# Key rows of a query block reordered to 32 keys, 24 summaries, 64 keys, in a fused window-attention and two-MoE-layer kernel

## Chip, core and metric

The kernel runs on one core of one Trainium2 chip. The metric is device microseconds of one execution, lower is better. Inputs and outputs are float32.

## What is computed

Attention over 2 batches of 8 heads with 768 tokens of 64 values each. A query sees the keys less than 16 tokens away, and 24 summaries: for each run of 32 tokens the maximum of its keys and the mean of its values. Two feed-forward layers follow. The reference, cut to what matters:

```python
block, window = (32, 16)
k_sum = k.reshape(B, H, nb, block, D).max(axis=3)
v_sum = v.reshape(B, H, nb, block, D).mean(axis=3)
scores_l = scale * np.matmul(q, k.transpose(0, 1, 3, 2))
mask_l = np.abs(pos[:, None] - pos[None, :]) < window
scores_s = scale * np.einsum('bhsd,bhnd->bhsn', q, k_sum) + np.log(block)
a = softmax(concat([where(mask_l, scores_l, -1e9), scores_s]))
x = a @ concat([v, v_sum])              # tokens x 512
h = np.maximum(x @ w_in, 0.0); x = h * h @ w_out
xn = rms_norm(x) * rms_g
out = (silu(xn @ w_gate) * (xn @ w_val)) @ w_out2
```

The weights arrive as float64 and are turned into float32 pairs on the chip.

## The kernel before

**Attention.** Tokens are worked on in 12 groups of 128 (6 to a batch), each as two query blocks of 64. For a block, 120 key rows are used: 96 keys of its window and the 24 summaries of its batch. `kT` holds the keys of a batch with the head dimension on the partitions; the rows of neighbouring blocks overlap in it, so that one slice of 120 columns is a block's whole key list. The list reads 16 keys, 12 summaries, 64 keys, 12 summaries, 16 keys: the two half sets of summaries alternate in the gaps between the blocks' keys. `vx` is the same list of values, with the 120 rows on the partitions and four slots, two blocks to a group.

For each group: `scores` (tiles `s`, PE), `softmax` (adding a mask, maximum, exponential, sum, scaling; tiles `t`, `mx`, `sm`; DVE and ACT), `ptrans` (transposes of `t` into `pps`, copied by ACT to `pT`), `av` (product with `vx` into `xps`), and `split_xs`, which makes from `xps` a rounded part `xhi` (ACT) and the rest `xlo` (DVE) for the next layer. A batch is prepared by `prep_k` (transposes of `kr` into `kps`, the maxima into `ksum` on DVE, a copy to `kT` on ACT), `prep_kend` (the summaries into the gaps of `kT`, DVE), `qprep` (`qr` through `qps` to `qT`) and `vmean` (24 means of the values from `vr` by a matmul, copied to `vm` on ACT).

**Values.** `vload` brings the keys' values of a group to `vx`, three DMAs to a block: 16, 64 and 16 rows. `vmfix` brings the means to the two 12-row places of each slot by DMA from `vm`, 4 DMAs for batch 0 and 8 for batch 1. All DMAs are issued from SP's queue, in order.

**Weights.** `Units` loads float64 weights (`raw_wi`, `raw_wo`, 512 KB each) and converts them: `conv_a` two ACT operations (L177, L178), `conv_b` four DVE operations (L184, L185, L188, L191), `split` one ACT cast (L197) and one DVE subtraction (L198). Of the first eight weight tiles, one is loaded near the start and seven are issued behind the first `vmfix` (`after("vmfix")`, L625).

**Order.** The program text gives the order of pieces; a scheduler then sets the instruction order of each engine, and each engine runs its instructions in that order. PE starts with batch 0's attention, then mixes the first feed-forward round (`h_pair` into tiles `h`, `y_pair` into tiles `y`, for token pairs `k_` of 256) with the attention of the later groups, to about 160 us; from there to the end it runs the feed-forward layers alone. Batch 1 is prepared in the round `k_ == 0`, and its means in the round `k_ == 1`, between `av(5)` and group 7.

Of the kernel before, what the change touches and what calls it, by code (L numbers as in the profile page):

```python
# [32 lines left out]
def tile_window_attention_moe_moe2(  # L33
# [25 lines left out]
    GAP = NB // 2  # L59
    NK = NB + KW  # L60
    STEP = QT + GAP
    NW1 = S // QT
    K0 = WIN + GAP
    K1 = K0 + STEP
    LK = WIN + (NW1 + 1) * GAP + S + WIN
# [31 lines left out]
    def constants():  # L97
# [33 lines left out]
        nc.gpsimd.memset(last[QT:P, K1:NK], NEG)  # L131
# [186 lines left out]
    def prep_k(b, c):  # L318
# [23 lines left out]
    def prep_kend(b, a):  # L342
        ksum = state[b]
        gaps = kT[:, :, WIN : WIN + NW1 * STEP].rearrange("d p (n s) -> d p n s", s=2 * STEP)
        half = ksum[:, :, GAP * a : GAP * (a + 1)]
        nc.vector.tensor_copy(
            gaps[:, :, :, STEP * a : STEP * a + GAP],
            half.unsqueeze(2).to_broadcast([P, NPAIR, NW1 // 2, GAP]),
        )
# [20 lines left out]
    def vmean(b, c):  # L370

        if c == 0:
            state["vmps"] = psA(f"vmean{b}", [NB, DM])
        ps = state["vmps"]
# [8 lines left out]
        if c == NC2 - 1:  # L383
            vm = ap_.tile([NB, DM], F32, tag="vm", name=f"vm{b}", bufs=1)
            nc.scalar.copy(vm, ps)
            state["vm"] = vm
            state[("vsum", b)] = True

    def vmfix(i0, n):

        vt = vx.rearrange("k (i u) h d -> k u i (h d)", u=2)
        for u in range(2):
            for j, a in ((WIN, u), (K0 + QT, 1 - u)):
                rows = state["vm"][GAP * a : GAP * (a + 1)]
                mark["vmfix"] = nc.sync.dma_start(
                    vt[j : j + GAP, u, i0 : i0 + n], rows.unsqueeze(1).to_broadcast([GAP, n, DM])
                )
# [300 lines left out]
    for k_ in range(NK2):  # L698
# [26 lines left out]
        if k_ == 0:  # L725
# [3 lines left out]
            prep_kend(1, 0)  # L729
            prep_kend(1, 1)  # L730
# [130 lines left out]
```

## Time and profile before

| | us |
|---|---|
| median of 3 runs | 676.23 |
| lowest, highest | 674.78, 677.02 |
| the profiled execution | 675.57 |
| its span on the core | 673.9 |
| PE busy in the span | 646.7 (96%) |
| DVE busy | 403.7 (60%) |
| ACT busy | 305.2 (45%) |
| POOL busy | 4.0 (1%) |

Engines: PE is TensorE, PEld its weight loads, DVE VectorE, ACT ScalarE, POOL GpSimd, SP the engine that issues the DMAs ("SPq" is its queue). Times count from the start of the span. An engine runs its instructions in order, so that one that waits holds up all behind it. The busy shares are means over stages: the first 125 us, where attention and the first feed-forward round mix, look different from the rest, and a change is to be read in its own stage. "PEclk" is the granted clock of PE as a share of 2.4 GHz; 0.50 is the level of 1.2 GHz.

### The profile page before, as it was taken

The numbers are of one execution on the slowest core, as the hardware profiler recorded it, in microseconds if no ns is written. First come the engines' busy times: TensorE is split into PE (matmuls) and PEld (weight loads), VectorE is DVE, ScalarE is ACT, GpSimd is POOL, SyncE is SP. The second block draws the span as 40 slices with busy tenths as digits, with TensorE's granted clock in tenths as the row PEclk, the third lists the DMA queues.
The fourth block names the chain that finished last, engine by engine and source line by source line (L and its number), as shares of the span: only waits on it lengthen the run. The fifth ranks groups of instructions, "written<-read, shape, count | busy, mean of one in ns | idle before, by whom it ended". The sixth has DMA issues, their size and how long they took to land.

```text
span 673.9 us, 9361 instructions
## 1 busy us (share of the span) xinstructions
PE 646.7 (96%) x3644; PEld 534.0 (79%) x3644; DVE 403.7 (60%) x733; ACT 305.2 (45%) x637; POOL 4.0 (1%) x25
## 2 busy tenths in 40 slices
PE   7668988999999999999999999999999999999997
PEld 5457957888888888888888888888888888888885
DVE  4799858565999669826665795189713172313132
ACT  4497558365775447416352773167511131111110
POOL 2000000000000000000000000000000000000000
PEclk9779998899999999999999999999999999999999
DMA  9677565221712314001022252014300000001011
GB/s 243 145 251 174 151 176 162 57 62 39 243 63 71 118 61 127 32 1 62 1 94 63 64 181 69 1 31 157 124 1 1 0 1 0 1 1 62 1 62 63
DMA packets 78188, 54.22 MB, mean 80 GB/s; under 512 B 46080, under 2 KB 72704, under 8 KB 78144
## 3 DMA queue, kind: packets, MB, share of 16 engines
q1 hardware_dynamic: 78144, 53.62, 26.9%
q8 instruction: 29, 0.48, 0.3%
q14 instruction: 15, 0.12, 0.1%
HBM read 50.07 MB, written 3.15 MB: 79 GB/s over the span
## 4 chain that ended last, share of the span: by engine, by line
PE 88%; SPq 4%; DVE 2%; DMA 2%; ACT 2%; issue 1%; DVEq 0%; ACTq 0%
PE y L532 19%; PE h L511 19%; PE v L511 15%; PE g L511 15%; PE z L532 14%; SPq L406 2%; PE xps L490 2%; PE s L420 2%; DMA raw_wi<-in_moe_w_in_dram 1%; PE pps L469 1%; SPq L305 1%; ACT t L449 1%; PE xps L502 1%; PE qps L366 1%; SPq L294 1%
## 5 line engine op out<-in xcount | busy, mean ns | idle before, releaser
L511 PE MATMUL h<-xhi,w_wi 128*128 128x512 f32 (+1 forms) x480 | 134.8, 354 | 2.5 <-ACT w_wi L197 1.7
L532 PE MATMUL y<-w_wo,hhi 128*128 128x512 f32 x384 | 119.8, 396 | 1.6 <-ACT hhi L522 1.4
L807 DVE TENSOR_TENSOR sg<-v,sg 128x512 f32<-128x512 f32 x36 | 24.8, 690 | 131.2 <-PE v L511 131.2
L511 PEld LDWEIGHTS h<-xhi,w_wi 128*128 128x128 f32 x480 | 86.5, 194 | 15.3 <-ACT w_wi L197 2.1
L511 PE MATMUL v<-xhi,w_wv 128*128 128x512 f32 x288 | 94.8, 390 | 0.0
L511 PE MATMUL g<-xhi,w_wg 128*128 128x512 f32 x288 | 94.6, 390 | 0.0
L532 PE MATMUL z<-w_wp,hhiz 128*128 128x512 f32 x288 | 88.1, 390 | 0.0
L511 PE MATMUL h<-xlo,w_wi 128*128 128x512 f32 (+1 forms) x240 | 85.2, 355 | 1.8 <-DVE xlo L481 1.8
L532 PEld LDWEIGHTS y<-w_wo,hhi 128*128 128x128 f32 x384 | 72.6, 191 | 16.9 <-ACT hhi L522 1.6
L532 PE MATMUL y<-w_wo,hlo 128*128 128x512 f32 x192 | 74.7, 399 | 0.0
L805 ACT ACTIVATE sg<-g 128x512 f32<-128x512 f32 x36 | 21.6, 599 | 102.3 <-PE g L511 100.0
L511 PEld LDWEIGHTS v<-xhi,w_wv 128*128 128x128 f32 x288 | 54.1, 188 | 11.2
L511 PEld LDWEIGHTS g<-xhi,w_wg 128*128 128x128 f32 x288 | 54.0, 188 | 11.1
L532 PEld LDWEIGHTS z<-w_wp,hhiz 128*128 128x128 f32 x288 | 54.0, 188 | 11.1
L659 ACT ACTIVATE r<-h 128x512 f32<-128x512 f32 x48 | 28.7, 597 | 66.2 <-PE h L511 65.9
L511 PE MATMUL v<-xlo,w_wv 128*128 128x512 f32 x144 | 56.1, 390 | 0.0
L511 PE MATMUL g<-xlo,w_wg 128*128 128x512 f32 x144 | 56.1, 389 | 0.0
L532 PE MATMUL z<-w_wp,hloz 128*128 128x512 f32 x144 | 55.4, 390 | 0.0
L522 ACT CAST hhiz<-sg 128x512 fp32r<-128x512 f32 x36 | 22.4, 621 | 68.3 <-DVE sg L807 68.0
L511 PEld LDWEIGHTS h<-xlo,w_wi 128*128 128x128 f32 x240 | 46.6, 194 | 8.4 <-DVE xlo L481 2.4
L660 DVE TENSOR_TENSOR r<-h,r 128x512 f32<-128x512 f32 x48 | 32.8, 684 | 33.0 <-ACT r L659 32.8
L532 PEld LDWEIGHTS y<-w_wo,hlo 128*128 128x128 f32 x192 | 36.2, 191 | 7.4 <-DVE mx L447 0.2
(125 smaller groups left out, 895.7 us busy)
## 6 DMA issues: line engine op xcount, KB each, us to landing
raw_wi<-in_moe_w_in_dram SPq DMA_DIRECT2D x16, 512.0 KB
raw_wo<-in_moe_w_out_dram SPq DMA_DIRECT2D x16, 512.0 KB
raw_wg<-in_moe_w_gate_dram SPq DMA_DIRECT2D x12, 512.0 KB
raw_wv<-in_moe_w_val_dram SPq DMA_DIRECT2D x12, 512.0 KB
raw_wp<-in_moe_w_out_dram SPq DMA_DIRECT2D x12, 512.0 KB
kr<-in_k_dram SPq DMA_DIRECT2D x12, 256.0 KB
qr<-in_q_dram SPq DMA_DIRECT2D x12, 256.0 KB
vr<-in_v_dram SPq DMA_DIRECT2D x6, 512.0 KB
```

The source lines that it names most:

```text
L294: nc.sync.dma_start(t.rearrange("p h e d -> p h (e d)"), src[b, :, 2 * P * c : 2 * P * (c + 1), :].rearrange("h (p e) d -> p h (e d)", e=2),)
L305: nc.sync.dma_start(t[:, j].rearrange("p (h d) -> p h d", h=H), src[b, :, o : o + P, :].rearrange("h p d -> p h d"),)
L406: nc.sync.dma_start(vx[j : j + n, i0 + u], v[b, :, o : o + n, :].rearrange("h s d -> s h d"))
L420: mark[("s", g)] = nc.tensor.matmul(sl[e][QT * u : QT * u + QT, p, :], qT[rr, p, QT * u : QT * u + QT], kT[rr, p, o : o + NK], start=True, ...
L490: nc.tensor.matmul(ps[QT * e : QT * e + QT, o : o + QT], vx[:, (2 * g + u) % NVX, 2 * p + e, :], pT[:, e * NPAIR + p, QT * u : QT * u + QT ...
L511: nc.tensor.matmul(ps, a_, b_, start=(i == 0), stop=(i == tot - 1))
L522: nc.scalar.copy(hi[:, 0:n], s[:, 0:n])
L532: nc.tensor.matmul(y, a_[:, ms], b_, start=(first and i == 0), stop=(last and i == 2))
L659: nc.scalar.activation(t, ps, AF.Relu)
L660: nc.vector.tensor_tensor(t, ps, t, op=ALU.mult)
L805: nc.scalar.activation(t, psg, AF.Silu)
L807: nc.vector.tensor_tensor(t, psv, t, op=ALU.mult)
```

## The change

A block's list of key rows becomes 32 keys, 24 summaries, 64 keys. The gaps of `kT` now hold all 24 summaries each. `prep_k` writes the keys with two ACT copies instead of one (12 more copies in all). `prep_kend` copies the summaries once on DVE for four blocks and once on POOL for eight (batch 0), or once on POOL for all twelve (batch 1). `vload` needs two DMAs to a block, of 32 and 64 rows. The means' rows stand in one place of `vx` (rows 32 to 55), so `vmean` is computed on those partitions and engines write the rows: DVE from PSUM for the first two slots of batch 0, POOL from `vm` for the others. The DMAs of `vmfix` are gone, and with them the order that put the seven weight loads behind them: these are now issued behind the second tile of queries. The masks follow the new order.

```diff
-            nc.scalar.copy(
-                kT[:, 2 * hf : 2 * hf + 2, K0 : K0 + NW1 * STEP]
-                .rearrange("d p (n s) -> d p n s", s=STEP)[:, :, nb1 * c : nb1 * (c + 1), 0:QT],
-                ps.rearrange("d p (n s) -> d p n s", s=QT),
-            )
+            nc.scalar.copy(kv[:, :, :, 0:WIN], pv[:, :, :, 0:WIN])
+            nc.scalar.copy(kv[:, :, :, WIN + NB : QT + NB], pv[:, :, :, WIN:QT])
...
+    def prep_kend(b, eng, w0, w1):
+        gaps = kT[:, :, WIN : WIN + NW1 * STEP].rearrange("d p (n s) -> d p n s", s=STEP)
+        eng.tensor_copy(
+            gaps[:, :, w0:w1, WIN : WIN + NB],
+            state[b].unsqueeze(2).to_broadcast([P, NPAIR, w1 - w0, NB]),
+        )
...
+            if b == 0:
+                nc.vector.tensor_copy(vrows(0, 2), ps.unsqueeze(1).to_broadcast([NB, 2, DM]))
             nc.scalar.copy(vm, ps)
...
+    def vmput(i0, n):
+        nc.gpsimd.tensor_copy(vrows(i0, n), state["vm"].unsqueeze(1).to_broadcast([NB, n, DM]))
...
-    prep_kend(0, 1)
+    prep_kend(0, nc.vector, 0, 4)
+    prep_kend(0, nc.gpsimd, 4, NW1)
...
-    vmfix(0, NVX // 2)
-    with after("vmfix"):
-        units1.load(8)
+    vmput(2, 2)
+    units1.load(8)
...
-            vmfix(0, 1)
+            vmput(0, 2)
...
-                vmfix(1, 1)
+                vmput(2, 2)
...
-            prep_kend(1, 0)
-            prep_kend(1, 1)
+            prep_kend(1, nc.gpsimd, 0, NW1)
```

**The start, SP's queue.** The rows show the end of the first loads of `vx` and the weights' issue, first before (`vm_292` are batch 0's means):

```order
L406 DMA vx<-in_v_dram 64x8x64
L406 DMA vx<-in_v_dram 16x8x64
L305 DMA qr_141<-in_q_dram 128x8x64 x2
L395 DMA vx<-vm_292 12x2x512 x4
L162 DMA raw_wi_298<-in_moe_w_in_dram 128x4x256
L162 DMA raw_wi_300<-in_moe_w_in_dram 128x4x256
L162 DMA raw_wi_302<-in_moe_w_in_dram 128x4x256
L166 DMA raw_wo_304<-in_moe_w_out_dram 128x1024
```

and in the changed kernel:

```order
L403 DMA vx<-in_v_dram 32x8x64
L403 DMA vx<-in_v_dram 64x8x64
L304 DMA qr_137<-in_q_dram 128x8x64 x2
L161 DMA raw_wi_296<-in_moe_w_in_dram 128x4x256
L161 DMA raw_wi_298<-in_moe_w_in_dram 128x4x256
L161 DMA raw_wi_300<-in_moe_w_in_dram 128x4x256
L165 DMA raw_wo_302<-in_moe_w_out_dram 128x1024
```

The four DMAs of the means are gone, the weights stand right behind the queries, and 8 loads of `vx` stand ahead of them instead of 12.

**Batch 1's means, SP's queue.** Before, from the end of the load of group 7's values (`vm_1093` are batch 1's means, `raw_wi_1515` and the rest the next weights):

```order
L406 DMA vx<-in_v_dram 16x8x64
L162 DMA raw_wi_1515<-in_moe_w_in_dram 128x4x256
L162 DMA raw_wi_1517<-in_moe_w_in_dram 128x4x256
L166 DMA raw_wo_1978<-in_moe_w_out_dram 128x1024
L395 DMA vx<-vm_1093 12x512 x8
L162 DMA raw_wi_1980<-in_moe_w_in_dram 128x4x256
L166 DMA raw_wo_1982<-in_moe_w_out_dram 128x1024
```

and in the changed kernel:

```order
L403 DMA vx<-in_v_dram 64x8x64
L161 DMA raw_wi_1493<-in_moe_w_in_dram 128x4x256
L161 DMA raw_wi_1495<-in_moe_w_in_dram 128x4x256
L165 DMA raw_wo_1954<-in_moe_w_out_dram 128x1024
L161 DMA raw_wi_1956<-in_moe_w_in_dram 128x4x256
L165 DMA raw_wo_1958<-in_moe_w_out_dram 128x1024
```

Eight DMAs between two weight loads are gone.

**The same place, ACT and DVE.** ACT before (`t_1015` is the softmax tile of group 6, `t_1123` that of group 7, `x_wi_1852` the first step on the second of the new weights):

```order
L480 CAST xhi_1_929<-xps_5_1067 128x4x128
L449 ACTIVATE t_1015,sm_1017<-t_1015,mx_1016 128x120 x8
L197 CAST w_wi_1856<-x_wi_1718 128x512
L177 ACTIVATE x_wi_1852<-raw_wi_1515 128x512
L385 COPY vm_1093<-vmean_1086 24x512
L178 ACTIVATE u_wi_1853<-raw_wi_1515 128x512
```

and now:

```order
L446 ACTIVATE t_1007,sm_1009<-t_1007,mx_1008 128x120 x8
L477 CAST xhi_1_923<-xps_5_1059 128x4x128
L384 COPY vm_1085<-vmean_1078 24x512
L196 CAST w_wi_1832<-x_wi_1694 128x512
L446 ACTIVATE t_1110,sm_1112<-t_1110,mx_1111 128x120 x8
L176 ACTIVATE x_wi_1828<-raw_wi_1493 128x512
```

The copy of the means and the exponentials of group 7 moved ahead of the new weights' first step. Some rows further on ACT, before (`pT_1295` are group 7's transposed weights of attention, `t_1243` is group 8's softmax tile):

```order
L659 ACTIVATE r_2_2_1333<-h_2_2_1308 128x512
L178 ACTIVATE u_wo_2025<-raw_wo_1982 128x512
L470 COPY pT_1295<-pps_0_1296 120x512
L470 COPY pT_1295<-pps_1_1302 120x512
L449 ACTIVATE t_1243,sm_1245<-t_1243,mx_1244 128x120 x8
```

and now:

```order
L177 ACTIVATE u_wo_2001<-raw_wo_1958 128x512
L467 COPY pT_1277<-pps_0_1278 120x512
L656 ACTIVATE r_2_2_1315<-h_2_2_1290 128x512
L446 ACTIVATE t_1225,sm_1227<-t_1225,mx_1226 128x120 x8
L467 COPY pT_1277<-pps_1_1284 120x512
```

The second half of group 7's `pT` moved behind the eight exponentials of group 8. DVE before, from the second add of group 6 to group 5's `xlo`:

```order
L443 TENSOR_TENSOR t_1015<-s_6_992,mask_first 128x480
L184 TENSOR_SCALAR x_wi_1718<-x_wi_1718 128x512
L447 TENSOR_REDUCE mx_1016<-t_1015 128x8
L185 TENSOR_SCALAR x_wi_1718<-x_wi_1718 128x512
L481 TENSOR_TENSOR xlo_1_930<-xps_5_1067,xhi_1_929 128x4x128
```

and now:

```order
L440 TENSOR_TENSOR t_1007<-s_6_986,mask_first 128x480
L444 TENSOR_REDUCE mx_1008<-t_1007 128x8
L440 TENSOR_TENSOR t_1110<-s_7_1088,mask_mid 128x480
L183 TENSOR_SCALAR x_wi_1694<-x_wi_1694 128x512
L184 TENSOR_SCALAR x_wi_1694<-x_wi_1694 128x512
L187 SCALAR_TENSOR_TENSOR x_wi_1694<-raw_wi_1491,x_wi_1694 128x512
L440 TENSOR_TENSOR t_1110<-s_7_1089,mask_mid 128x480
L190 ISA x_wi_1694<-x_wi_1694,u_wi_1695 128x1024
L444 TENSOR_REDUCE mx_1111<-t_1110 128x8
L454 TENSOR_SCALAR sm_1009<-sm_1009 128x8
L478 TENSOR_TENSOR xlo_1_924<-xps_5_1059,xhi_1_923 128x4x128
```

Group 5's `xlo`, which the next `h` products need, moved behind both adds and the maximum of group 7; on PE the means' matmuls stand between the two halves of group 7's scores.

## Rows read from the trace of the kernel before

**Rows 1.** The page: busy time, and the granted clock in 40 slices.

```profile
PE 646.7 (96%) x3644; PEld 534.0 (79%) x3644; DVE 403.7 (60%) x733; ACT 305.2 (45%) x637; POOL 4.0 (1%) x25
PEclk9779998899999999999999999999999999999999
```

**Rows 2.** The page: the chain that ended last, shares by engine.

```profile
PE 88%; SPq 4%; DVE 2%; DMA 2%; ACT 2%; issue 1%; DVEq 0%; ACTq 0%
```

**Rows 3.** By stage, us busy: PE, PEld, DVE, ACT, POOL; then clock, DMA share, GB/s.

```profile
20.00:28.00 8.00, 2.46 (x11) 1.93 (x10) 7.76 (x20) 3.87 (x14) 0.00 (x0) 0.80 0.54 121
28.00:38.00 10.00, 10.00 (x148) 8.55 (x147) 5.21 (x11) 6.74 (x23) 0.00 (x0) 0.82 0.83 272
38.00:52.00 14.00, 8.12 (x40) 7.27 (x38) 13.60 (x28) 12.47 (x35) 0.00 (x0) 0.64 0.74 204
52.00:70.00 18.00, 15.64 (x198) 12.97 (x198) 18.00 (x33) 13.06 (x34) 0.00 (x0) 1.00 0.77 182
70.00:88.00 18.00, 18.00 (x149) 15.65 (x148) 12.46 (x21) 10.29 (x19) 0.00 (x0) 1.00 0.54 129
...
98.00:100.40 2.40, 0.41 (x4) 0.16 (x3) 0.56 (x2) 1.25 (x3) 0.00 (x0) 1.00 1.06 390
...
110.00:112.50 2.50, 0.69 (x5) 0.45 (x5) 2.50 (x4) 1.26 (x3) 0.00 (x0) 1.00 1.05 329
112.50:124.50 12.00, 12.00 (x82) 9.68 (x83) 8.34 (x13) 7.16 (x23) 0.00 (x0) 0.57 0.49 133
124.50:160.00 35.50, 35.50 (x352) 31.23 (x352) 17.59 (x28) 18.64 (x55) 0.00 (x0) 1.00 0.19 46
```

**Rows 4.** Timeline of SP's queue: start, duration, DMAs of a run.

```profile
13.66 8.72 SPq L406 DMA_DIRECT2D vx<-in_v_dram  x12
22.42 1.06 SPq L305 DMA_DIRECT2D qr<-in_q_dram  x2
...
29.39 1.61 SPq L162 DMA_DIRECT2D raw_wi<-in_moe_w_in_dram  x3
...
90.18 4.34 SPq L406 DMA_DIRECT2D vx<-in_v_dram  x6
94.62 0.94 SPq L162 DMA_DIRECT2D raw_wi<-in_moe_w_in_dram  x2
...
100.29 6.27 SPq L395 DMA_DIRECT2D vx<-vm  x8
106.68 0.49 SPq L162 DMA_DIRECT2D raw_wi<-in_moe_w_in_dram  x1
```

**Rows 5.** Waits from 56 to 130 us: total, times, longest.

```profile
ACT u_wi L178 <- DMA raw_wi<-in_moe_w_in_dram: 2.3, 1, 2.3
...
PE pps L469 <- ACT vm L385: 2.0, 1, 2.0
```

**Rows 6.** Timeline of PE and ACT at three places.

```profile
26.10 1.09 PE L366 MATMUL qps<-ident,qr 128*128 128x128 f32 x4 [5.54 <-DMA qr<-in_q_dram]
...
90.54 5.33 PE L379 MATMUL vmean<-vr,ind 128*24 128x512 f32 x12
...
99.15 0.66 ACT L177 ACTIVATE x_wi<-raw_wi 128x512 f32<-128x512 f32 x1 [3.09 <-DMA raw_wi<-in_moe_w_in_dram]
```

**Rows 7.** Groups by line and shape: busy, mean ns of one.

```profile
L449 ACT ACTIVATE t<-t,mx 128x120 f32<-128x120 f32 x72 | 27.4, 384 | 8.5 <-DVE mx L447 8.5
...
L447 DVE TENSOR_REDUCE mx<-t 128x8 f32<-128x960 f32 x7 | 8.0, 1146 | 0.1
...
L336 ACT COPY kT<-kps 128x512 f32<-128x512 f32 x12 | 7.0, 586 | 7.5 <-DVE ksum L331 7.5
...
L346 DVE COPY kT<-ksum 128x288 f32<-128x288 f32 x4 | 1.2, 308 | 0.1
...
L125 POOL COPY mask_mid<-um 64x16 f32<-64x16 f32 x2 | 0.4, 194 | 0.1
...
L127 POOL COPY mask_first<-mask_mid 128x120 f32<-128x120 f32 x1 | 0.3, 282 | 0.1
```

More of the change, by code (lines that the diff above doesn't have):

```diff
@@ L58, in tile_window_attention_moe_moe2 @@
     KW = QT + 2 * WIN
-    GAP = NB // 2
     NK = NB + KW
-    STEP = QT + GAP
+    STEP = QT + NB
     NW1 = S // QT
-    K0 = WIN + GAP
-    K1 = K0 + STEP
-    LK = WIN + (NW1 + 1) * GAP + S + WIN
+    G0 = 2 * WIN
+    K1 = G0 + NB
+    LK = NW1 * STEP + G0
     GPB = S // P
@@ L122, in constants @@
         nc.gpsimd.memset(mid, math.log(BLK))
-        for j, n, o in ((0, WIN, 0), (K0, QT, WIN), (K1, WIN, WIN + QT)):
+        for j, n, o in ((0, G0, 0), (K1, QT, G0)):
             nc.gpsimd.tensor_copy(mid[0:QT, j : j + n], um[0:QT, o : o + n])
@@ L130, in constants @@
         nc.gpsimd.tensor_copy(last, mid)
-        nc.gpsimd.memset(last[QT:P, K1:NK], NEG)
+        nc.gpsimd.memset(last[QT:P, NK - WIN : NK], NEG)
         masks.update(first=first, mid=mid, last=last)
@@ L335, in prep_k @@
             )
-            nc.scalar.copy(
-                kT[:, 2 * hf : 2 * hf + 2, K0 : K0 + NW1 * STEP]
-                .rearrange("d p (n s) -> d p n s", s=STEP)[:, :, nb1 * c : nb1 * (c + 1), 0:QT],
-                ps.rearrange("d p (n s) -> d p n s", s=QT),
-            )
[L342 to L348, printed above, removed]
-        )
-        if a == 0:
-            nc.vector.tensor_copy(kT[:, :, WIN + NW1 * STEP : WIN + NW1 * STEP + GAP], half)
+            kv = kT[:, 2 * hf : 2 * hf + 2, WIN : WIN + NW1 * STEP].rearrange(
+                "d p (n s) -> d p n s", s=STEP
+            )[:, :, nb1 * c : nb1 * (c + 1)]
+            pv = ps.rearrange("d p (n s) -> d p n s", s=QT)
+            nc.scalar.copy(kv[:, :, :, 0:WIN], pv[:, :, :, 0:WIN])
[5 more added lines that the diff above has]
+            state[b].unsqueeze(2).to_broadcast([P, NPAIR, w1 - w0, NB]),
+        )
     def vm_load(b, c):
@@ L372, in vmean @@
         if c == 0:
-            state["vmps"] = psA(f"vmean{b}", [NB, DM])
-        ps = state["vmps"]
+            state["vmps"] = psA(f"vmean{b}", [K1, DM])
+        ps = state["vmps"][G0:K1]
         pb = BLK // 2
@@ L383, in vmean, with vrows @@
         if c == NC2 - 1:
-            vm = ap_.tile([NB, DM], F32, tag="vm", name=f"vm{b}", bufs=1)
+            vm = ap_.tile([K1, DM], F32, tag="vm", name=f"vm{b}", bufs=1)[G0:K1]
+            state["vm"] = vm
+            if b == 0:
+                nc.vector.tensor_copy(vrows(0, 2), ps.unsqueeze(1).to_broadcast([NB, 2, DM]))
             nc.scalar.copy(vm, ps)
[L386 to L397, printed above, removed]
+    def vrows(i0, n):
+        return vx[G0:K1, i0 : i0 + n].rearrange("k i h d -> k i (h d)")
+    def vmput(i0, n):
+        nc.gpsimd.tensor_copy(vrows(i0, n), state["vm"].unsqueeze(1).to_broadcast([NB, n, DM]))
     def vload(g):
@@ L403, in vload @@
             t0 = r * P + u * QT
-            for j, n, o in ((0, WIN, t0 - WIN), (K0, QT, t0), (K1, WIN, t0 + QT)):
-                o = min(max(o, 0), S - n)
+            rows = [
+                (0, G0, t0 - WIN) if t0 else (WIN, WIN, 0),
+                (K1, QT, t0 + WIN) if t0 + QT < S else (K1, QT - WIN, t0 + WIN),
+            ]
+            for j, n, o in rows:
                 nc.sync.dma_start(
@@ L611, in tile_window_attention_moe_moe2 @@
         nc.gpsimd.memset(kT[:, :, j : j + WIN], 0.0)
+    nc.gpsimd.memset(vx[0:WIN, 0], 0.0)
     prep_k(0, 0)
@@ L614, in tile_window_attention_moe_moe2 @@
     prep_k(0, 1)
-    prep_kend(0, 0)
     prep_k(0, 2)
     qprep(0)
-    prep_kend(0, 1)
+    prep_kend(0, nc.vector, 0, 4)
+    prep_kend(0, nc.gpsimd, 4, NW1)
     scores(0)
```

## The prediction

> **What bounds the kernel now.** The page comes first: PE is busy 96% of the span and carries 88% of the chain that ended last [rows 1, 2]. What can still be saved is the time in which PE waits, and the time at the lower clock. Each slice of the clock is 673.9 / 40 = 16.8 us, and only four stand below 9: the second and third (17 to 51 us) and the seventh and eighth (101 to 135 us) [rows 1]. So the next view is busy time by stage [rows 3]. From 124.5 us on PE is busy without a gap at full clock: what is gained or lost before that point goes to the end unchanged, and the whole question lies in the first 125 us.
>
> Three stages there lose time. From 20 to 28 us PE is busy 2.46 of 8.00 us: it waits 5.54 us for the second tile of queries [rows 6], which SP issued at 22.42, behind twelve loads of values [rows 4]. From 28 to 38 us PE works, but DVE only 5.21 of 10.00 us: the weights that it could convert were issued at 29.39, behind the means' DMAs [rows 4]. And from 38 to 70 us DVE is the bound (13.60 of 14.00, then 18.00 of 18.00 us) while PE idles 5.88 and 2.36 us, the first with its clock at 0.64 [rows 3]. The idle of DVE in the stage before is thus paid later.
>
> The third loss stands around batch 1's means. From 98.0 to 100.4 us every engine stands nearly still (PE 0.41, DVE 0.56 of 2.40 us) [rows 3]: ACT waits 3.09 us for a weight tile [rows 6] that SP could issue only at 94.62, behind group 7's values [rows 4]; the copy of the means sits behind it in ACT's order, and PE waits 2.0 us for that copy, since it frees a PSUM tile [rows 5]. From 110.0 to 112.5 PE is busy 0.69 of 2.50 us: ACT again waits, 2.3 us, for a weight tile [rows 5], which SP issued at 106.68, after 6.27 us of the means' DMAs [rows 4]. Then PE runs 12.00 us at a clock of 0.57 [rows 3].
>
> **The change, part by part.** I make the sum against the profiled execution, 675.57 us; the median of the runs shown is 0.66 above it.
>
> *Start.* Four of twelve loads of `vx` go. Twelve took 8.72 us, 0.73 each [rows 4], so the queries are issued at most 2.9 us earlier, and not at all if the time goes with the rows moved; I take 2.4, as the loads that remain are few rows longer. The four DMAs of the means went between 23.5 and 29.39, so the weights are issued about 8 us earlier, near 21. Their data can flow: the DMA engines are busy 0.54 from 20 to 28 us [rows 3]. DVE can then convert in its idle time of 28 to 38 us, 10.00 - 5.21 = 4.79 us. DVE's own work changes by the copy of the means from PSUM, 1024 columns (1.15 us for 960, so 1.2 [rows 7]), and one copy of 384 summaries (0.31 for 288, so 0.4), against two of 0.31 and a smaller one that go: 0.8 more. So the stage in which DVE is the bound ends 4.79 - 0.8 = **4.0 us** earlier; bounds 0 (DVE's or ACT's order wastes the time) and 4.8. That PE follows is read from the stages: its idle of 5.88 and 2.36 us there is more than the gain.
>
> *Copies on ACT.* Twelve more, at 0.1 us (the part of 0.586 that does not grow with the columns, were it small) to 0.4 (an exponential of 120 columns, 0.384 [rows 7]). Six stand at the start, where the scores would come 0.1 to 0.4 us later, and DVE is then busy with the first weight; six in the stage from 70 to 88 us, where ACT is busy 10.29 of 18.00 us [rows 3]. I take nothing; without that cover it would be 0.4 at each place.
>
> *Copies on POOL.* The trace has POOL copies of 16 columns at 0.194 and of 120 at 0.282 us [rows 7], a slope of 0.85 ns a column. By it 768, 1024 and 1152 columns take 0.8, 1.05 and 1.15 us; the strided and repeated reads could double that. POOL has no other work by then, nothing stands behind the copies on it, and the readers come later: batch 0's summaries are ready before 12 us and first read behind the queries' wait; of batch 1's, PE runs at least 4 us of `y`, `xps` and `qps` products between the last transposes of keys and the scores; the means of batch 1 are read by group 6's `xps` after two whole `h` tiles. I take nothing; lower bound nothing, upper 1 us where batch 1's summaries are read.
>
> *Batch 1's place, removed.* The eight DMAs (6.27 us) no longer stand before the weights, and group 7's values are four DMAs instead of six (4.34 us for six). The weight that came at 94.62 is then bound by the slot that the means' matmuls free, and ACT comes to it later, behind the copy of the means and eight exponentials (3.1 us). So both waits on weights go: 2.40 - 0.41 = 1.99 and 2.50 - 0.69 = 1.81 us, and if the clock stays up, 12.00 x (1 - 0.57) = 5.16. Together **8.96 us**.
>
> *Batch 1's place, added.* The scheduler's new order costs two waits. Group 5's `xlo` now stands on DVE behind the second add of group 7, which waits for scores that PE makes after 5.33 us of means [rows 6]. From those scores to `xlo` DVE needs an add (0.6, half of 1.15), a step of a weight (0.6), the maximum (1.15 [rows 7]) and `xlo` (0.6), 2.95 us; PE has two `h` products, 0.4, meanwhile: a new wait of 2.5 us, bounds 1 and 3. And the second half of group 7's `pT` stands on ACT behind eight exponentials, 8 x 0.384 = 3.1 us; PE has some half a microsecond of scores: 2.6, bounds 0 and 3. Two such waits may bring the clock down again. After the wait of 98 to 100.4 alone it stayed up; after the second, at 110 to 112.5, it fell for 12 us. So this costs 0 to 5.16 us, and neither row decides; I take half, 2.6. Net: 8.96 - 2.5 - 2.6 - 2.6 = **1.3 us** saved, bounds -2.2 (3 + 3 + 5.16 against 8.96) and 8.0.
>
> *Sum.* 4.0 + 1.3 = 5.3 us. 675.57 - 5.3 = 670.3 for the profiled execution, and with the 0.66 us to the median **670.9 us**.
>
> **A rule that speaks against the change.** No row shows POOL and DVE at work on large tiles at once; POOL is busy 4.0 us in all, at the start [rows 1]. The Trainium skill, "SBUF — State Buffer", section "Who interferes with whom", says that a GpSimd instruction and a DVE instruction that reads two SBUF operands, or runs in a two-port mode, lock each other out for the whole instruction. No run here shows it yet; as a mechanism of this kernel it is the third rival below.
>
> **Rivals.**
> 1. *The waits at batch 1 vanish and the clock stays up.* For it: each new wait is worked out from DVE's and ACT's orders on the assumption that PE arrives early, and PE held full clock through the waits of 52 to 70 us [rows 3]. Then 4.0 + 8.96 less one wait of 2.5: 665.8 us (663.3 with no new wait at all).
> 2. *Both new waits stand and the clock falls as before.* 2.5 + 2.6 + 5.16 against 8.96 is -1.3, so only the start's gain is left: 676.23 - 4.0 + 1.3 = 673.5.
> 3. *POOL and DVE hold each other up.* Three copies of means fall where DVE is wanted (after batch 0's means, and two ahead of group 5's `xlo`): 3 x 1.05 = 3.2 us that DVE stands, 670.9 + 3.2 = 674.1.
> 4. *ACT stalls on weights at the start, and the kernel is slower.* ACT works in order, and the steps of the second weight now stand ahead of the second half of group 0's `pT`, the exponentials of group 2 and `xhi`. Should the tile land late, as the one at 94.62 did (ACT got it 4.5 us later [rows 4, 6]), all of that stands still. ACT comes to it at about 27 us; each microsecond of landing after that is one of loss, the gain of 4.0 is gone at 31, and with landing at 36 (fifteen after issue, behind all that is issued around it) the time is 676.23 + 9 - 4.0 - 1.3 = 680. Against it: DMA at 0.54 in that stage, and a landing of 4.5 us gives 25.5.
>
> That the loads do not come earlier at all is excluded by SP's order, unless the queries' tile itself is not earlier, which is in the bounds.
>
> **How the numbers follow.** The forecast (668 to 672.5) has 0.42, rival 1 0.27, rival 2 0.17, rival 3 0.07, rival 4 0.07. The most likely case gives 670.9. The range from 664.5 to 677.0 leaves out rival 4 and the best end of rival 1. About 0.3%, 2 us, is what a measurement of this kernel can tell from no change: faster is below 674.2. All of the forecast and of rival 1, and a little over half of rivals 2 and 3 (0.13), are faster: 0.82. The rest of these, 0.11, is the same; rival 4, 0.07, is slower.
>
> **What would show each step right or wrong.** Start: the first weights' issue near 21 us, DVE busy above 8 of 10 us from 28 to 38, and the stage in which DVE is never idle ending near 66 instead of 70 us. Wrong, if ACT shows waits on `raw_wi` before 40 us. Batch 1: no wait of ACT on weights between 85 and 120 us, no wait of PE on `vm`; in their place a wait of `h` on `xlo` after the means and one of `xps` on `pT`, and the clock after them tells rivals 1 and 2 apart. POOL: copies near 1 us, no reader that waits on POOL, and DVE instructions beside them no longer than their groups. The prediction is wrong altogether if PE shows new idle time after 125 us, since I let the whole difference before it through to the end.

## The result, and the profile after

The changed kernel takes 668.84 us (median of 4 runs, 668.43 to 669.63) against 675.68 beside it: a ratio of 0.9899, 95% interval 0.9878 to 0.9919. Forecast were 670.9 us, 664.5 to 677.0, and faster; the gain of 6.8 us is 1.5 us larger than the 5.3 of the sum. Measured a second time (label c0 below) it took 668.29 us, a ratio of 0.9932 (0.9904 to 0.9959). The changed kernel hardly moved; the kernel before is what spreads, 669 to 677 us, and a part of this document is on why.

The page of the changed kernel, which answers to [rows 1, 2]: busy time, the clock in 40 slices, the chain.

```profile
PE 647.4 (97%) x3644; PEld 535.2 (80%) x3644; DVE 402.6 (60%) x729; ACT 306.5 (46%) x649; POOL 10.2 (2%) x29
PEclk8969999999999999999999999999999999999999
PE 90%; DVE 4%; ACT 2%; DMA 1%; SPq 1%; issue 1%; DVEq 0%; ACTq 0%
```

Busy time by stage, the columns of [rows 3]:

```profile
28.00:38.00 10.00, 6.70 (x77) 5.14 (x75) 9.94 (x26) 9.29 (x28) 0.00 (x0) 0.71 1.08 362
38.00:52.00 14.00, 13.29 (x109) 11.94 (x109) 14.00 (x29) 12.50 (x34) 0.00 (x0) 0.72 0.83 186
52.00:70.00 18.00, 18.00 (x211) 15.85 (x208) 17.67 (x31) 11.54 (x31) 0.00 (x0) 1.00 0.39 101
...
96.00:102.00 6.00, 5.26 (x32) 5.26 (x33) 5.14 (x13) 5.95 (x21) 0.00 (x0) 0.72 0.04 16
```

From 28 to 38 us DVE is now busy 9.94 of 10.00 us (5.21 before), and PE's idle of 5.88 us from 38 to 52 has shrunk to 0.71; from 52 to 70 PE, not DVE, is the one without a gap. At batch 1's place the clock stands at 0.72 for six microseconds where it stood at 0.57 for twelve.

SP's queue of the changed kernel, which answers to [rows 4]:

```profile
14.09 7.02 SPq L403 DMA_DIRECT2D vx<-in_v_dram  x8
21.15 1.25 SPq L304 DMA_DIRECT2D qr<-in_q_dram  x2
22.45 2.38 SPq L161 DMA_DIRECT2D raw_wi<-in_moe_w_in_dram  x3
```

Its PE and ACT around batch 1's means, and POOL's copies:

```profile
87.25 5.33 PE L375 MATMUL vmean<-vr,ind 128*24 128x512 f32 x12
96.74 0.39 PE L508 MATMUL h<-xlo,w_wi 128*128 128x256 f32 x1 [2.76 <-DVE xlo L478]
115.42 1.15 PE L487 MATMUL xps<-pT,vx 120*64 120x64 f32 x30 [1.59 <-ACT pT L467]
...
92.67 0.58 ACT L384 COPY vm<-vmean 24x512 f32<-24x512 f32 x1 [0.36 <-PE vmean L375]
107.53 0.67 ACT L177 ACTIVATE u_wi<-raw_wi 128x512 int32<-128x512 uint32 x1 [1.52 <-DMA raw_wi<-in_moe_w_in_dram]
...
25.20 1.51 POOL L390 COPY vx<-vm 24x1024 f32<-24x1024 f32 x1 [13.13 <-ACT vm L384]
93.38 2.48 POOL L390 COPY vx<-vm 24x1024 f32<-24x1024 f32 x2 [13.98 <-ACT vm L384]
```

The means of batch 1 start on PE at 87.25 us (90.54 before [rows 6]), and both forecast waits stand: 2.76 us of `h` on group 5's `xlo`, 1.59 us of `xps` on group 7's `pT`. The old two, of ACT on a weight ahead of the copy to `vm` and of PE on `vm`, are gone; the copy now follows the means at once.

**How the gain divides.** I take the start of batch 1's means as a mark: what lies ahead of it is the start, what lies behind it batch 1's place and the rest. Two traces of each kernel (before: the first and label c1; after: the first and c0) give

| | means start | span less that |
|---|---|---|
| before | 90.54, 90.65 | 583.4, 581.6 |
| after | 87.25, 85.95 | 579.9, 579.4 |

so 4.0 us of gain at the start (forecast 4.0) and 2.8 us behind it (forecast 1.3). c0's row of the means is

```profile
85.95 5.33 PE L375 MATMUL vmean<-vr,ind 128*24 128x512 f32 x12
```

Two things blur the division. The mark does not stand behind quite the same work: 16 of group 7's score matmuls come ahead of it in the changed kernel (at 85.21 us, 0.96 us until the next row), while all of them come behind it before (at 95.80 us). By equal work the division is nearer to 5.0 and 1.8 us. And the two traces of the changed kernel differ by 1.3 us in the mark, as much as in the start of SP's first value loads (14.09 and 12.80 us), which stands ahead of all that was changed. Counted from there the means start after 73.2 us in both, and after 76.9 and 77.5 us in the kernel before.

### The profile page after: what moved, and what is told of

Read it like the earlier page. It is cut to its first block, busy times and chain, and to the rows that moved or that the text cites. A ratio compares the mean times of both kernels' runs of the same rounds, so it can differ in the third digit from the quotient of the medians.

```text
span 667.1 us, 9349 instructions
## 1 busy us (share of the span) xinstructions
PE 647.4 (97%) x3644; PEld 535.2 (80%) x3644; DVE 402.6 (60%) x729; ACT 306.5 (46%) x649; POOL 10.2 (2%) x29
## 4 chain that ended last, share of the span: by engine, by line
PE 90%; DVE 4%; ACT 2%; DMA 1%; SPq 1%; issue 1%; DVEq 0%; ACTq 0%
PE y L529 19%; PE h L508 19%; PE v L508 15%; PE g L508 15%; PE z L529 14%; PE s L417 2%; PE vmean L375 2%; PE xps L487 2%; PE pps L466 1%; ACT t L446 1%; SPq L304 1%; DMA qr<-in_q_dram 1%; PE xps L499 1%; DVE mx L444 1%; DVE t L440 1%
## 5 line engine op out<-in xcount | busy, mean ns | idle before, releaser
L529 PE MATMUL y<-w_wo,hhi 128*128 128x512 f32 x384 | 118.0, 392 | 0.6 <-ACT hhi L519 0.6
L529 PEld LDWEIGHTS y<-w_wo,hhi 128*128 128x128 f32 x384 | 71.2, 188 | 15.1 <-ACT hhi L519 0.9
```

Source lines behind the costliest of these rows:

```text
L529: nc.tensor.matmul(y, a_[:, ms], b_, start=(first and i == 0), stop=(last and i == 2))
```

## The experiments

The theory was: the start's gain comes from weights that are issued early and fill DVE's idle time; batch 1's gain comes from the eight DMAs of the means that no longer stand ahead of weights; the two new waits give a part of it back. Each is timed beside the kernel before on its own chip; c1 is a single execution, for its trace.

| label | median us | ratio to before, 95% |
|---|---|---|
| c0_after_again | 668.29 | 0.9932 [0.9904, 0.9959] |
| e1_before_weights_early | 681.01 | 1.0110 [1.0073, 1.0148] |
| e2_after_weights_held | 669.93 | 0.9955 [0.9930, 0.9980] |
| e3_after_three_loads | 671.33 | 0.9971 [0.9948, 0.9994] |
| e4_after_means_by_dma | 669.19 | 0.9942 [0.9918, 0.9966] |
| e8_batch0_means_by_dma | 668.30 | 0.9925 [0.9903, 0.9946] |
| e5c_xlo_ahead | 665.70 | 0.9885 [0.9849, 0.9922] |
| e6_pool_busy | 669.33 | 0.9946 [0.9922, 0.9970] |
| f1_before_vm_ahead | 670.04 | 0.9960 [0.9938, 0.9982] |
| e9_queries_ahead | 666.50 | 0.9915 [0.9888, 0.9942] |
| e10_means_by_pool | 668.62 | 0.9945 [0.9924, 0.9966] |

**c0: the changed kernel again**, with no edit.

> The changed kernel itself, unchanged, beside the kernel before on the same chip and beside the three others of this call. If the kernel before spreads by chip and start as in the calls so far (674.8 to 677.0, then 669.4 to 677.1 us), the ratio lies between 0.9899 and 0.995; if the gain is one of a single chip's state, it is nearer to 1.

The ratio lies where the first case put it. The kernel before was at 672.88 us here (25 runs, 668.95 to 676.52), 2.8 us below the 675.68 of the result; the changed kernel was 0.55 us below its 668.84.

### The start

**e1: early weights alone, in the kernel before.**

```
-    with after("vmfix"):
-        units1.load(8)
+    units1.load(8)
```

> The kernel before (675.6 us) with one part of the change alone: the seven weight loads no longer stand behind the means' DMAs of batch 0, but behind the second tile of queries; key list, twelve value loads and all DMAs of the means stay. Theory (the start's gain comes from weights that reach DVE early): first of the three weights issued near 23.5 instead of 29.39 us, DVE busy above 8 of 10 us from 28 to 38 us (5.21 before), PE's first scores of group 6 near 83 instead of 87.15 us, 671 to 673 us in all. Rival (the start's gain comes from the shorter queue ahead of the queries, which this kernel lacks): DVE may fill, but group 6 starts no earlier than 86.5 us, 675 to 676 us. Rival (the gain is another instruction order at batch 1 alone): group 6 at 87, 671 to 673 us.

It is slower by 1.1%, and DVE is busy 5.95 of 10 us from 28 to 38 us, where I had expected more than 8. SP, ACT and PE of this run:

```profile
23.31 2.13 SPq L162 DMA_DIRECT2D raw_wi<-in_moe_w_in_dram  x3
43.14 3.77 SPq L395 DMA_DIRECT2D vx<-vm  x4
...
30.31 0.66 ACT L177 ACTIVATE x_wi<-raw_wi 128x512 f32<-128x512 f32 x1 [5.41 <-DMA raw_wi<-in_moe_w_in_dram]
33.07 0.56 ACT L385 COPY vm<-vmean 24x512 f32<-24x512 f32 x1
...
33.68 1.11 PE L469 MATMUL pps<-ident,t 128*120 128x128 f32 x4 [5.46 <-ACT vm L385]
47.05 1.12 PE L490 MATMUL xps<-pT,vx 120*64 120x64 f32 x16 [5.91 <-DMA vx<-vm]
```

The weights were issued at 23.31 us as expected, but ACT's order put their first step ahead of the copy to `vm`. ACT stood 5.41 us on a tile that had not landed, PE 5.46 us on the copy, and the means' DMAs, now behind queries and keys in SP's queue, came so late that group 0's product waited 5.91 us more. That is the prediction's fourth rival, in another kernel: here early weights did not pay without means that need neither SP nor a place behind a weight on ACT.

**e3: three value loads to a block again.**

```
+            j, n, o = rows[0]
+            if n == G0:
+                rows = [(j, WIN, o), (j + WIN, WIN, o + WIN), rows[1]]
```

> The changed kernel with the 32-row load of each block cut into two of 16 rows, so that SP issues three loads to a block again (eleven instead of eight at the start); the other engines' orders are the same. Theory (SP's time ahead of queries and weights is what counts, and goes with the number of DMAs, 0.73 us each): queries and weights issued 2.2 us later (23.3 and 24.6 us), group 6 starts 1 to 2 us later than at 82.43, and the total is 669.8 to 671 us. Rival (SP's time goes with the rows, not with the DMAs): queries stay near 21.2 us and the total at 668.8. Rival (the queries' place alone makes the start's gain): PE's wait for them returns to 4 us or more, 672 to 673.5 us.

The loads began 1.5 us earlier here than in the first trace of the changed kernel (12.64 for 14.09 us), so I compare with e4 (12.97). Eleven loads took 8.27 us where the eight of e4, otherwise the same program up to there and run on the same chip, took 6.35; queries and weights went out 1.6 us later (20.95 and 22.24 against 19.36 and 20.65), the means started at 87.39 against 86.02, 1.4 us later, and the medians are 2.1 us apart. So SP's time went with the DMAs, as expected, and by the means and the medians it came through. The two traced executions end together (spans of 667.0 and 667.4 us), e3's being the fastest of its twelve.

**e9: queries ahead of the value loads** (with the order of e5c).

```
-    vload(0)
-    vload(1)
     qload(2)
+    vload(0)
+    vload(1)
```

> The changed kernel with group 5's xlo ahead of group 7's adds (the run with xlo ahead gave 665.7 us) and the second tile of queries issued ahead of the eight value loads instead of behind them. Theory (what is left of the start's loss is PE's wait for those queries, 2.1 to 2.7 us, and the low clock behind it; from 28 to 70 us DVE is the bound, so that little more than DVE's idle of 20 to 38 us, 1 to 1.5 us, can come back): queries issued near 13 instead of 20 us, no wait of PE for them, total 664 to 665 us. Rival (the clock counts more than DVE's idle): 661 to 663 us. Rival (DVE's bound swallows it, or the values' later loads hold up group 0's product): 665.5 to 667 us.

SP's queue, then the stage from 28 to 38 us:

```profile
13.07 2.93 SPq L304 DMA_DIRECT2D qr<-in_q_dram  x2
...
23.55 1.72 SPq L161 DMA_DIRECT2D raw_wi<-in_moe_w_in_dram  x3
```

```profile
28.00:38.00 10.00, 7.23 (x70) 5.82 (x70) 8.57 (x22) 7.98 (x22) 0.00 (x0) 0.50 1.06 361
```

No gain: 666.50 us, 0.8 us above e5c on another chip, as the last rival had it. PE no longer waits for these queries. They went out 7 us earlier than in e5c (20.23) and the weights 2.0 us later (21.52 there); DVE is busy 8.57 of 10 us (9.38 in e5c) and the means start at 88.53, 1.65 us later than e5c's 86.88. In this pair the earlier queries did not make up for the later weights; as both moved at once, the run doesn't price either.

**e2 and e8: weights behind batch 0's means again**, with two DMAs for slots 2 and 3 (e2), or with four for all slots and no copy on DVE (e8):

```
-    vmput(2, 2)
-    units1.load(8)
+    for i in (2, 3):
+        mark["vmfix"] = nc.sync.dma_start(vrows(i, 1)[:, 0], state["vm"])
+    with after("vmfix"):
+        units1.load(8)
```

> The changed kernel (668.8 us) with the weights put back behind batch 0's means: for the slots 2 and 3 the means go by two DMAs instead of one POOL copy, and the seven weight loads stand behind them; queries stay early, batch 1 stays as changed. Theory (early weights make the start's gain): weights issued near 28 us, DVE 5 to 6 of 10 us busy from 28 to 38 us, group 6's scores start 3.5 to 4.5 us later than in the changed kernel (82.43), and the total is 672 to 673.5 us. Rival (the early queries make it): group 6 within 1.5 us of 82.43, total 669 to 670 us. The order at batch 1 differs here too (group 5's xlo stands ahead of group 7's adds), which can take up to 2.8 us off either number.

```
-            if b == 0:
-                nc.vector.tensor_copy(vrows(0, 2), ps.unsqueeze(1).to_broadcast([NB, 2, DM]))
...
+        for i in (0, 2):
+            mark["vmfix"] = nc.sync.dma_start(
+                vrows(i, 2)[NB // 2 * a : NB // 2 * (a + 1)],
```

> The changed kernel with batch 0's means written as before the change, by four DMAs from vm into 12 rows of two slots each, and the seven weight loads behind them; neither DVE nor POOL writes means of batch 0; eight value loads, so queries stay early; batch 1 as changed. Theory (the weights wait behind the means, and that made the start's loss): weights issued near 28 us (22.45 in the changed kernel, 25.40 with two DMAs ahead of them), DVE under 8 of 10 us busy from 28 to 38 us, the means of batch 1 start on PE 2 to 3.5 us later than at 87.25, total 670.5 to 673 us. Rival (queries and eight loads make the start's gain): batch 1's means within 1 us of 87.25, total within 1 us of the changed kernel's.

The weights went out at 25.40 (e2) and 25.48 us (e8), earlier than I had expected since the means' DMAs took only 1.72 and 3.48 us. The stage from 28 to 38 us in e2, then in e8:

```profile
28.00:38.00 10.00, 6.47 (x103) 5.24 (x99) 9.14 (x21) 8.22 (x26) 0.00 (x0) 0.88 1.08 386
```

```profile
28.00:38.00 10.00, 10.00 (x94) 8.39 (x90) 6.98 (x15) 8.00 (x26) 0.00 (x0) 0.50 1.08 387
```

With the same times of issue DVE is busy 9.14 of 10 us in one and 6.98 in the other, and the means start at 86.22 and 88.86. The theory's 2 to 3.5 us stand in e8 (2.9 behind c0's 85.95, though 1.6 behind the 87.25 that I had counted from) and not in e2. The totals, 669.93 and 668.30 us, lie where the rivals had them, but do not decide, since the order at batch 1 differs in both as well. The instruction orders of the first 90 us differ in the two; the issue of the weights is thus not the whole cause. The kernel before says the same: its first weight behind the means, issued at 29.39, was first touched by ACT at 37.49 without a wait,

```profile
37.49 0.68 ACT L177 ACTIVATE x_wi<-raw_wi 128x512 f32<-128x512 f32 x1
```

so there it was ACT's order that left DVE idle, not a tile that had not landed. What may make e8's total equal to c0's is told under e5c.

**e10: DVE's copy of the means given to POOL** (with the order of e5c).

```
-            if b == 0:
-                nc.vector.tensor_copy(vrows(0, 2), ps.unsqueeze(1).to_broadcast([NB, 2, DM]))
...
+    vmput(0, 2)
     vmput(2, 2)
```

> The changed kernel with group 5's xlo ahead of group 7's adds (665.7 us), and batch 0's means of slots 0 and 1 written by POOL from vm instead of by DVE from PSUM, so that DVE has one copy of 1.22 us less at the start. Theory (from 28 to 70 us DVE is the bound, and what is taken from it there or just ahead of it comes back in full): batch 1's means start 0.8 to 1.4 us earlier than at 86.88 us, total 664.3 to 665 us. Rival (POOL's second copy, 1.2 to 1.5 us, comes late for group 0's product, or DVE's idle grows by the time taken from it): 665.5 to 667 us. The scheduler's order of the first 90 us differs too, by which either can come out a microsecond off.

Slower than e5c, by 2.9 us of medians on different chips. DVE has 1.13 us of idle from 38 to 52 us that e5c has not (12.87 of 14.00 busy), and new waits stand at batch 1's place (2.26 us of `y` on `hhi`, 2.02 us of `pps` on `xlo`). The means do start earlier, at 84.09 us, by 2.8 us where 0.8 to 1.4 were expected; but 0.8 of that stands already in the start of the value loads (12.80 for 13.58), and about 1 us in score matmuls of group 7 that come behind the means in this order. What is left, 1 us, would fit the theory; the total doesn't show it. The orders differ from e5c's everywhere, so the run doesn't price the copy; it is inconclusive on that.

### Batch 1's place

**e4: batch 1's means by eight DMAs again**, between the same two weights; every other engine's order is that of the changed kernel.

```
-            vmput(0, 2)
+            vmdma(0, 2)
...
-                vmput(2, 2)
+                vmdma(2, 2)
```

> The changed kernel with batch 1's means written by eight DMAs on SP's queue, between the same two weight loads as before, instead of two POOL copies; the other engines' orders are the same. Theory (the means' DMAs ahead of the weights made the second wait and the loss of clock there): the weights behind them are issued 5 to 6 us later (near 109 instead of 103.2 us), ACT waits for them 5 us or more (1.5 us now) with group 7's pT behind it, PE waits 3 to 5 us more and its clock falls: 672 to 677 us. Rival (what was gained there came from the new order of ACT and DVE alone, and the weights are early enough anyway): 668.3 to 669.8 us.

The rival's numbers: 669.19 us, the ratio within 0.001 of c0's. ACT and SP:

```profile
91.45 0.58 ACT L384 COPY vm<-vmean 24x512 f32<-24x512 f32 x1 [0.62 <-PE vmean L375]
...
92.05 6.34 SPq L396 DMA_DIRECT2D vx<-vm  x8
101.85 0.39 SPq L161 DMA_DIRECT2D raw_wi<-in_moe_w_in_dram  x1
```

The eight DMAs take their 6.34 us as before, but they start right behind the copy to `vm`, at 92.05, and end 3.5 us before the next weight is issued at all (101.85; 101.92 in c0, without them). So the DMAs by themselves cost nothing that the ratio shows: my theory on this place fell.

**f1: two ACT instructions exchanged in the kernel before.** The copy to `vm` goes ahead of the first step on the second new weight; every other order is the same.

```
-            nc.scalar.copy(vm, ps)
+            mark[f"vm{b}"] = nc.scalar.copy(vm, ps)
...
+                with after(*(["vm1"] if u == ("wi", 5) else [])):
                     self.a[u] = conv_a(self.raw.pop(u), "%s%d" % u)
```

> The kernel before with two ACT instructions exchanged and nothing else: the copy of batch 1's means to vm now stands ahead of the first step on the second of the new weights (x_wi), where it stood behind it; every other engine's order is the same. Theory (batch 1's loss hangs on that order: the copy sat behind a weight that had not landed, and the eight means' DMAs and the weights behind them on SP went late with it): the means' DMAs are issued 3 us earlier (near 97 instead of 100.29 us, when PE's means start at 90.54), PE's wait on vm (2.0 us) goes, ACT's second wait on a weight (2.3 us) shrinks, PE's clock stays up behind it; the total is 2 to 6 us below the kernel before, ratio 0.991 to 0.997. Rival (the eight DMAs themselves, 6.27 us on SP, are the loss wherever they stand): within 1 us of the kernel before.

2.45 us faster than before by the medians (1.2 to 4.2 by the interval), with its runs between 668.88 and 672.09 us. The timeline of ACT and SP, then two of the stages of [rows 3] at this place:

```profile
96.84 0.57 ACT L386 COPY vm<-vmean 24x512 f32<-24x512 f32 x1
99.29 0.67 ACT L177 ACTIVATE x_wi<-raw_wi 128x512 f32<-128x512 f32 x1 [1.88 <-DMA raw_wi<-in_moe_w_in_dram]
...
97.43 6.28 SPq L396 DMA_DIRECT2D vx<-vm  x8
103.83 0.45 SPq L162 DMA_DIRECT2D raw_wi<-in_moe_w_in_dram  x1
```

```profile
98.00:100.40 2.40, 2.40 (x22) 2.29 (x20) 1.06 (x4) 1.11 (x2) 0.00 (x0) 1.00 1.07 380
112.50:124.50 12.00, 12.00 (x121) 10.72 (x119) 10.66 (x17) 7.42 (x25) 0.00 (x0) 1.00 0.28 78
```

ACT still waits 1.88 us for the weight, but the copy no longer stands behind it. PE works through 98 to 100.4 us without a gap, the means' DMAs go out 2.9 us earlier, ACT's second wait of 2.3 us is gone, and the clock stays at 1.00. Behind the start of its means (91.20) f1 needs 576.8 us, less than the changed kernel's 579.4 to 579.9: the changed kernel removes the same loss and pays its two new waits.

**e5c: group 5's `xlo` ahead of group 7's adds.**

```
+                with after(("xlo", g, 1)):
+                    group(g + 2)
+                vmput(2, 2)
```

> The changed kernel with group 5's xlo ahead of group 7's adds on DVE (group 7 is issued behind it); the scheduler then also puts group 6's pT and the weights' first steps ahead of group 7's exponentials on ACT. Theory (the wait of h on xlo, 2.76 us, and the clock that falls behind it, about 1.7 us, are a price of the changed order): the wait goes, the clock stays at 1.00 from 96 to 102 us, and the total is 2 to 4.5 us below the changed kernel's (664.5 to 667 where that stands at 668.8). Rival (PE has nothing else to do there, the wait turns into one on group 7's t or group 6's pT): within 1 us of the changed kernel.

2.6 us below c0 on the same chip, 664.77 to 667.29 us against 666.65 to 669.82: as the theory has it, and the fastest of all kernels here. The stage behind the means in c0, then in e5c:

```profile
96.00:102.00 6.00, 6.00 (x36) 6.00 (x35) 5.13 (x12) 5.76 (x17) 0.00 (x0) 0.60 0.00 1
```

```profile
96.00:102.00 6.00, 4.88 (x63) 4.43 (x61) 5.14 (x11) 6.00 (x23) 0.00 (x0) 1.00 0.13 22
```

PE is less busy in e5c and yet starts more matmuls (63 for 36), at full clock. The wait on `xlo` is gone; four shorter ones stand in its place (0.68, 0.54, 1.05 and 1.57 us, between 98 and 108.4 us), so the rival is right in part. The 2.6 us are in the medians and not in these two executions: their spans are 665.3 and 665.6 us, c0's the second fastest of nine, e5c's the slowest of six. Behind the start of its means e5c needs 578.7 us and e9, with the same order there, 576.7, where the changed kernel needs 579.4 and 579.9. The orders of the engines differ from c0's between 85 and 214 us, so this is the gain of the new order as a whole, in which `xlo` is what was set.

In e8, too, the scheduler put `xlo` ahead. That may have made up for what its start lost, but it is not shown: its one trace, the slowest of its eleven runs, needs 579.7 us behind the means.

### POOL, and the kernel before once more

**e6: POOL kept busy.** Twelve dead copies behind each copy of means; every other order is the same.

```
+        for i in range(12):
+            nc.gpsimd.tensor_copy(edge[G0:K1], state["vm"][:, 0:120])
```

> The changed kernel with twelve more POOL copies of 24x120 behind each of the three copies of means (36 in all, read from vm, written to a spare tile); the orders of the other engines are the same. Theory (POOL is off every path and does not hold DVE up): 0 to 0.5 us more than the changed kernel, DVE's instructions beside POOL no longer than in their groups by 5 per cent. Rival (POOL and DVE lock each other out): POOL is busy some 7 to 9 us more, most of it beside DVE's work at 26 to 30 and 94 to 100 us, DVE's instructions there stretch, and the total rises by 2 to 6 us.

The dead copies take 17.3 us on POOL, 13.1 of them in one stretch from 94.4 us, and the median is 1.0 us above c0's, with intervals that overlap: more than the theory's 0.5, less than the rival's 2. DVE from 93 to 108 us in c0, then in e6 (columns as in [rows 7]):

```profile
L187 DVE SCALAR_TENSOR_TENSOR x_wi<-raw_wi,x_wi 128x512 uint32<-128x512 uint32 x2 | 1.3, 682 | 0.0
L444 DVE TENSOR_REDUCE mx<-t 128x8 f32<-128x960 f32 x1 | 1.1, 1139 | 0.0
```

```profile
L187 DVE SCALAR_TENSOR_TENSOR x_wi<-raw_wi,x_wi 128x512 uint32<-128x512 uint32 x2 | 1.5, 764 | 0.0
L446 DVE TENSOR_REDUCE mx<-t 128x8 f32<-128x960 f32 x1 | 1.1, 1139 | 0.0
```

Some of DVE's instructions get 82 to 87 ns longer beside POOL, whatever their length (0.682 to 0.764 us here, 0.418 to 0.505 at L183), and the maximum doesn't. That is more than the 5 per cent I had allowed, but it is POOL that waits. Its dead copies, shortest, median and longest in ns:

```profile
L392 POOL COPY edge<-vm x36: 278/360/1218, 24.9 to 107.3; 24x120 f32<-24x120 f32 x36
```

A copy takes 278 ns beside a maximum, or beside an add that reads scores from PSUM. Beside an instruction of DVE that reads SBUF alone, reductions apart, it ends 135 to 146 ns behind that instruction, at the longest 1218 ns beside the scaling of `t` at 98.06 us. The Trainium skill, "SBUF — State Buffer", section "Who interferes with whom", has the later of the two blocked until the other's instruction ends. POOL's copies agree with that. It also says that a reduction never contends on this chip, and the unchanged 1139 ns agree with that.

**c1: the kernel before, a second trace.**

> The kernel before, unchanged, for a second trace: its runs spread from 669 to 677 us, those of the changed kernel from 666.7 to 669.8. If the spread comes from batch 1's place (ACT's wait for a weight ahead of the copy of the means, by the luck of the DMA queues), the waits at 98 to 100 and 110 to 112 us and the clock behind them differ from those of the first trace by as much as the totals do; if it comes from the start, the means of batch 1 start at another time than 90.54.

The means on PE, then three of the stages of [rows 3]:

```profile
90.65 5.33 PE L379 MATMUL vmean<-vr,ind 128*24 128x512 f32 x12
```

```profile
98.00:100.40 2.40, 0.92 (x9) 0.68 (x7) 1.03 (x4) 1.66 (x4) 0.00 (x0) 1.00 1.05 382
110.00:112.50 2.50, 0.98 (x5) 0.71 (x6) 2.50 (x4) 1.55 (x3) 0.00 (x0) 1.00 1.08 292
112.50:124.50 12.00, 11.88 (x89) 9.59 (x88) 8.20 (x13) 6.87 (x23) 0.00 (x0) 0.72 0.44 124
```

The means start within 0.11 us of the first trace. The span is 1.7 us shorter (672.2 for 673.9), and the clock from 112.5 to 124.5 us, 0.72 where it was 0.57 [rows 3], makes at most 12 x 0.15 = 1.8 us. The two waits are a little shorter as well (1.48 and 1.52 us of idle PE in their stages for 1.99 and 1.81). Counted from the means, c1 is 0.4 us ahead at the `y` product behind the second wait (112.17 us for 112.47) and 1.8 us ahead at the `h` product that follows these (122.67 for 124.33). So some 0.4 us is the waits, and 1.4 us is the low clock, which lasts less long behind them.

The spread goes with the clock: of the 25 runs of the kernel before beside c0, the three fastest (669.0 to 669.7 us) have a mean granted clock of 0.986 to 0.987, the three slowest (675.2 to 676.5 us) one of 0.978 to 0.979. That all of it is lost at this place two traces don't show; f1, without the low clock there, spreads over 3.2 us.

## Why the prediction was right, and where it was off

**Start, 4.0 us: size right, reason half right.** The two traces of each kernel give 4.0. DVE's idle filled as said (9.94 of 10 us). But the queries went out at 21.15 and 19.79 us in the two traces (20.0 forecast) and the weights at 22.45 and 21.08 (near 21). The step that fails is the one from issue to use. I took the late issue for the cause of the idle, while in the kernel before ACT came to the weight only 8.1 us after its issue, without waiting. The change moved the weights on SP, and the scheduler, which saw them earlier, moved their steps on ACT and DVE; e3 shows that the issue counts, and e9 fits that; e2 and e8 point to the order.

That the size came out is in part luck. In c1 ACT reached the first of these weights at 35.70 us instead of 37.49, and DVE was busy 7.00 of 10 us instead of 5.21, yet the means start no earlier (90.65 for 90.54). So the idle time of DVE from which I worked out the 4.0 does not set the gain by itself.

One sign I had tied to the bounds of a stage: that DVE would cease to be always busy near 66 us instead of 70. Its first wait behind 52 us, before and in the changed kernel:

```profile
77.12 0.69 DVE L331 TENSOR_REDUCE ksum<-kps 128x16 f32<-128x512 f32 x1 [0.34 <-PE kps L328]
69.11 0.69 DVE L542 COPY yp<-y 128x512 f32<-128x512 f32 x1 [0.33 <-PE y L529]
```

In c1 it stands ahead of 72.56 us, in c0 ahead of 67.80. So the stretch does end earlier, by 3 to 9 us, though neither end lies where I had it; and PE no longer waits for DVE from 52 to 70 us (18.00 us busy for 15.64).

**Copies on ACT and POOL, nothing: no row against it.** POOL took 1.51 and 1.24 us for 1024 columns of means (1.05 forecast) and no row of PE or DVE waits on it. The twelve more ACT copies were not tried apart.

**Batch 1, removed 8.96 us: right waits, wrong cause for one, and a clock term that is no constant.** The waits at 98 and 110 us went. ACT waits for weights at two other points between 85 and 120 us, where I had forecast none: 1.52 us at 107.53, and 2.91 us ahead of 87.58 (0.99 at 90.17 before), while PE is busy without a gap. I had put the second wait down to the means' DMAs; e4 has them back at no cost that the ratio shows, and f1 removes the loss with the DMAs in place. In the kernel before they held up the second weight because they themselves started late, behind the copy to `vm`. What mattered is that ACT's copy to `vm` no longer sits behind a weight's first step, which the prediction named for the first wait only. Of the 8.96, 5.16 was the clock of one execution. The second trace gives 1.48 + 1.52 + 12 x 0.28 = 6.4.

**Batch 1, added 7.7 us: both waits there, one mis-sized.** `h` on `xlo` took 2.76 us in both traces (2.5 forecast), the clock behind it 5.26 x 0.28 = 1.5 and in c0, from 95.44 to 101 us, 5.56 x 0.48 = 2.7 us (2.6 forecast). `xps` on `pT` took 1.59 and 0.33 us (2.6 forecast): PE had more other work than the half microsecond that I had counted, and this term is most of the miss in c0; in the first trace the clock's term misses by as much. With 5.9 and 5.8 added, the place nets 0.5 to 3.2 us by the waits, 2.8 by the mark of the means (some 1.8 by equal work), against 1.3.

**Sum.** 4.0 + 2.8 is 6.8 us between the spans, 5.3 forecast. By c0's medians the gain is 4.6 us, since the kernel before was 2.8 us faster there and the changed one 0.55. PE's new idle time after 125 us, by which the prediction was to be wrong altogether, is 0.63 us at 132.48 us, against two waits of 0.24 and 0.22 us that went (162.35 and 163.07): too little to count.

**Rivals.** The first two (no new waits and full clock; both waits and the clock as before) bracket what came. The third, POOL and DVE holding each other up at 3.2 us, is refuted by e6 in that size: 17.3 us of POOL, where the copies of means take 4.0, cost about 1 us. In the changed kernel itself the step of DVE that meets two of these copies, at 94.17 us, takes 0.785 us, where the same step takes at most 0.693 elsewhere. The fourth did not happen in the changed kernel, where ACT's only wait on `raw_wi` from 20 to 40 us is one of 0.31 us in c0 (at 26.93 us), but e1 shows that it was a real danger.

## What to carry to other kernels

A short copy that frees a buffer or feeds a queue should not stand behind an instruction that waits for a transfer: exchanging two ACT instructions was worth 2.45 us here, half of the 4.6 us that the whole change gained by c0's medians. When a change takes DMAs off a queue, ask which instruction order the scheduler makes of it before crediting the DMAs; put them back alone, as e4 did, and see. And a wait in the middle of matmuls is to be priced with the clock behind it, as a range, since behind much the same waits PE lost some 1.4 us more to the clock in one execution than in another.

## What the runs showed of the hardware

- The low clock behind much the same waits lasted differently in two executions of one program: 0.57 and 0.72 over the same twelve microseconds. That was some 1.4 us of time.
- DVE beside POOL (e6): DVE's instructions that were held were longer by 82 to 87 ns in the mean. POOL waited more: a copy of 24x120 took 278 ns at the least and 1218 at the most, ending 135 to 146 ns behind the instruction of DVE that held it, and a copy of 1024 columns took 1.51 us at 23.45 us and 1.03 at 91.77.
- From issue to ACT's first use a weight tile needed 7.0 us in e1 (23.31 to 30.31, ACT waiting), and 4.2 us in e8 (25.48 to 29.71, ACT waiting), with the DMA engines busy 0.75 and 0.66 of their time from 20 to 28 us and 1.03 and 1.08 from 28 to 38 us.
